# Two of 24 triangular inverses moved from VectorE elimination through DRAM to block doubling on TensorE

## The chip, the cores and the metric

The kernel runs on one core of a Trainium2 chip. A core has five engines that each work through their own instruction stream in order and wait for each other through semaphores: TensorE (PE, with its weight loads PEld), VectorE (DVE), ScalarE (ACT), GpSimd (POOL) and SyncE (SP). SP, ACT and POOL also issue DMAs; a DMA that must wait holds everything behind it in that engine's stream. The metric is the device time in microseconds, where lower is better.

## The reference

Two blocks follow each other. The first is a recurrence (RWKV-7) over 768 tokens for 4 batches and 8 heads with head size 40:

```python
for t in range(S):
    y[:, :, t] = np.einsum('bhd,bhde->bhe', rt, state)
    Sa = np.einsum('bhde,bhe->bhd', state, at)
    state_decay = state * wt[:, :, None, :] - np.einsum('bhd,bhe->bhde', Sa, bt)
    state = state_decay + np.einsum('bhd,bhe->bhde', vt, kt)
```

The second takes the 3072 x 320 result `x` through a feed-forward block: `h = x @ w_in` (1024 wide), `solu = h * softmax(h)`, a layer norm over the 1024 values with gain `g_ln`, and `@ w_out` back to 320. The inputs `w_in`, `w_out` and `g_ln` come as float64 and the kernel gets the two matrices as 64-bit integers.

## The kernel before, in words

The recurrence is cut into chunks of 64 tokens. Within a chunk the effect of `a` and `b` of earlier tokens on later ones is a unit triangular 64 x 64 system for each batch and head, and the chunk needs its inverse. A *step* handles one chunk of two batches, so 16 such systems: there are 24 steps, even ones for batches 0 and 1, odd ones for batches 2 and 3. The systems of a step are independent of the recurrent state, so they can be prepared ahead.

Preparing step i takes, in the order of the code: `load_keys` (w, b, a, k from DRAM), `decay` (L288, logarithm, cumulative sum on PE, two exponentials), `decay_turned` (transposition into `ex`), `scaled` (POOL multiplies b or k by the inverse decay), `front` (L330, transposed `aT`, made by DVE, and `bT`, made by ACT) and `norm` (L351, 16 products on PE, masked by DVE into `nt`, the strictly triangular matrices, and written to DRAM as `nt_dram`).

The inverse is made for a *group* of two steps by `invert` (L379). It reads the two 32 x 32 diagonal blocks of all 32 matrices back from DRAM in another layout (`blk`, `spread`, L370), one block per partition and half, and eliminates column by column on DVE: 30 pairs of a multiply (`prod`, L392) and a subtract (`uu`, L394), each over 128 partitions. The result goes to DRAM (`uu_dram`), and `bring` (L403) loads it back per step as `tu` (one diagonal block) and `uh` (the other). `flip` (L415, a DVE transpose), `couple` (L421, PE product `py`, ACT copy `wy`) and `close` (L434, PE product `pz`, ACT copy into `tu`) then make the full 64 x 64 inverse in `tu[:, :, 32:96]`.

A step's main part follows: `scores` (products of keys, masked by DVE into `psi` and `lv`), `driven` (`px`, the right-hand side), `solved` (`pu`, times the inverse), `answered` (`pl`, masked into `lu`), `read` (`pyo`, output and new state), `leave` (scaling by DVE, and DMAs that turn the output into `xT`). Two to four steps later the feed-forward block of the same tokens runs: `hidden` (product `h`), `exped`, `weighed`, `spreadof`, `folded`, `output`.

The weights are turned from 64-bit floats to 32-bit by DVE and ACT: `land` brings 18 pieces in 13 loads, `narrow(n)` converts the next n pieces (L177 to L191, seven DVE and two ACT instructions a piece). All 18 must be done before `centre_w2` (L207), which runs in step 4.

The order of PE, POOL, DVE and SP is the order of the code. `some(n)` lets n pairs of the oldest unfinished inverse run at that place on DVE. The main loop (L763) starts at i = -1; its body i prepares step i + 5 and does the main part of step i and `scores`, `couple` and `close` of step i + 1. A group takes 30 pairs, so 15 per step are needed; `shares` (L761) and `narrowed` (L762) say where the pairs and the conversions stand in the first bodies. Before the loop the code prepares steps 0 to 3 and does the whole elimination of group 0 (steps 0 and 1, `some(8)`, `some(8)`, `some(14)`) with four conversions among it.

PSUM has three pools: `banks` (two buffers of two banks), `h` (one buffer of two banks) and `bank` (two buffers).

Of the kernel before, what the change touches and what calls it, by code (L numbers as in the profile page):

```python
# [16 lines left out]
P = 128  # L17
# [6 lines left out]
LAG = 1  # L24
LN_EXP = "natural_log_exp_and_others"


def shape_constants():
    s, t = np.arange(P)[:, None], np.arange(P)[None, :]
    same = s // C == t // C  # L30
    row = np.arange(P)[:, None] % C
    parts = dict(
        ident=np.eye(P),
        cum=same & (s <= t),
        tri=row < np.arange(C)[None, :],
        eye_hi=row == Q + np.arange(Q)[None, :],
        neg_hi=-(row >= Q).astype(np.float64),
        mean=np.full((P, P), 2.0 ** -10),
    )
    at, where = 0, {}  # L40
    for name, x in parts.items():
        where[name] = (at, at + x.shape[1])
        at += x.shape[1]
    return np.concatenate([np.asarray(x, np.float64) for x in parts.values()], 1).astype(np.float32), where


@with_exitstack
def kernel(
# [49 lines left out]

    ident, tri = c_("ident"), c_("tri")
# [188 lines left out]
    def decay(i):  # L288
        if not ok(i):
            return  # L290
        d = st[i]
        lw = two.tile([P, DM], FP32, tag="lw", name="lw", bufs=1)
        nc.scalar.activation(out=lw, in_=d["raw_w"].rearrange("p h d -> p (h d)"), func=AF.Ln)
        t = (bank("pcum") if i > 5 else ps2.tile([P, DFF], FP32, tag="h", name="h"))[:, 0:DM]
        nc.tensor.matmul(t, lhsT=c_("cum"), rhs=lw, start=True, stop=True)  # L295
        nc.scalar.activation(out=ei_t[0][:, :, 0:D], in_=heads(t), func=AF.Exp)
        inv = d["inv"] = two.tile([P, DM], FP32, tag="inv", name="inv", bufs=4)
        nc.scalar.activation(out=inv, in_=t, func=AF.Exp, scale=-1.0)
# [52 lines left out]
    def norm(i):  # L351
# [9 lines left out]
        masked(nt, t[:, :, 0:256])  # L361
        n, at = divmod(i, GRP)
# [6 lines left out]

    def spread(n):  # L370
        nb = two.tile([P, Q, Q], FP32, tag="blk", name="blk")
        for y in range(2):
            for e in range(2):
                home = C * y + Q * e
                queue = nc.gpsimd if y and not n else nc.sync
                queue.dma_start(out=nb[home:home + Q], in_=blocks[n][:, Q * e:Q * e + Q, Q * e:Q * e + Q])
# [26 lines left out]
    def bring(i):  # L403
        if not ok(i):
# [10 lines left out]
    def flip(i):  # L415
        if not ok(i):
# [4 lines left out]
    def couple(i):  # L421
        if not ok(i):
# [11 lines left out]
    def close(i):  # L434
        if not ok(i):
# [268 lines left out]
    for i in range(2):  # L704
        load_keys(i, "w")
        load_keys(i, "b", nc.scalar)
        load_keys(i, "a")
    nc.scalar.dma_start(out=g_rows, in_=moe_g_ln.rearrange("(c p) -> c p", p=P))
    load_keys(2, "w")
    for n in range(3):  # L710
        land(n, nc.sync)
    decay(0)
    decay_turned(0)
    for i in range(4):
        scaled(i, "b")
        if i == 3:
            scaled(0, "k")
            scaled(1, "k")
# [4 lines left out]
        if i == 0:  # L723
            load_keys(2, "ba")
        if i == 1:
            load_keys(3, "w")
            begin_inverse(0)
            narrow(3)
            load_keys(3, "ba")
            load_keys(0, "k")  # L730
            load_keys(4, "w")
            some(8)
        if i == 2:
            load_values(0)
            load_keys(1, "k")
            some(8)
    load_keys(5, "w")
    load_keys(4, "ba")
    begin_inverse(1)
    for i in (2, 3):  # L740
        load_keys(i, "k", nc.gpsimd)
    by_value(0)
# [6 lines left out]
    land(3, nc.sync)  # L749
    some(14)  # L750
    narrow(1)
    bring(0)
# [8 lines left out]
    shares = {-1: (0, 8, 6), 0: (0, 9, 7), 1: (0, 9, 6), 2: (0, 9, 6), 3: (0, 9, 6)}  # L761
    narrowed = {-1: (0, 2), 0: (1, 2), 1: (1, 3), 2: (1, 2), 3: (1, 1)}  # L762
    for i in range(-1, N + 3 + LAG):  # L763
# [20 lines left out]
        attend_kv(i + 1)  # L784
        hidden(m - 2, ((1, 1),))
        attend_rs(i + 1)
# [20 lines left out]
        scores(i + 1)  # L807
        if i < 0:
            flip(i + 1)
# [41 lines left out]
```

## Time and profile before

| what | value |
|---|---|
| time, median of 3 runs | 663.46 us (662.66 to 665.79) |
| the profiled execution, its own time | 663.51 us |
| its span, first to last instruction | 661.7 us |
| PE busy | 572.6 us (87%) |
| PEld busy | 408.2 us (62%) |
| DVE busy | 490.0 us (74%) |
| ACT busy | 238.9 us (36%) |
| POOL busy | 216.4 us (33%) |
| elimination pairs on DVE, 12 groups | 108.8 + 107.8 us |
| mean granted TensorE clock | 0.903 |

Busy shares are means over the whole span; the first 200 us and the rest have different limits, so stretches of the span and the chain of waits are read one by one. A row of the timeline has the start, the duration, the engine, the line, the operation and its tiles; a bracket gives the idle time of the engine just before it and what ended that. Matrix products of this kernel are of 32-bit floats and appear as two records each, so 16 products are `x32`.

### The profile page before, as it was taken

To read this page: it belongs to the slowest core of one execution; us is meant where nothing else is said; L and a number is where in the kernel's file an instruction comes from. 1 tells how busy PE (TensorE), PEld (TensorE's weight loads), DVE (VectorE), ACT (ScalarE), POOL (GpSimd) and SP (SyncE) were. 2 spreads that over 40 slices of the span, in tenths; PEclk is the share of its full clock that TensorE was granted. 3 is DMA by queue.
4 is the path that set the end of the run, shared out by engine and by line. 5 is a ranking of instruction groups with operands and counts; after the bars stand their busy time and mean duration, and the time that the engine had idled before them with its cause. 6 is when DMAs were issued, how large, how long until landed. Compare 5 with 4: busy or idle time off the path is not lost.

```text
span 661.7 us, 26730 instructions
## 1 busy us (share of the span) xinstructions
PE 572.6 (87%) x11449; PEld 408.2 (62%) x11449; DVE 490.0 (74%) x1344; ACT 238.9 (36%) x494; POOL 216.4 (33%) x384
## 2 busy tenths in 40 slices
PE   5246674778698999999999999999999999999995
PEld 3134553665565767766776677667766767666653
DVE  4777977888995978888879788888797888423431
ACT  4213333333341443444344334433443233332221
POOL 2342304155050444144315431543244313422200
PEclk9565668659598999999999999999999999999998
DMA  8958976456343645455466465553442412310000
GB/s 165 159 101 132 169 136 106 108 106 124 62 87 62 114 84 108 90 112 107 87 109 114 85 114 89 108 108 77 75 86 58 96 39 48 70 36 26 23 20 20
DMA packets 276749, 59.93 MB, mean 91 GB/s; under 512 B 264656, under 2 KB 274488, under 8 KB 276632
## 3 DMA queue, kind: packets, MB, share of 16 engines
q1 hardware_dynamic: 263384, 44.96, 38.9%
q0 software_dynamic: 7856, 8.76, 5.5%
q10 hardware_dynamic: 5392, 4.51, 2.4%
q8 instruction: 90, 1.47, 0.9%
q14 instruction: 27, 0.22, 0.1%
HBM read 40.10 MB, written 13.37 MB: 81 GB/s over the span
## 4 chain that ended last, share of the span: by engine, by line
PE 73%; DVE 12%; DMA 6%; issue 3%; ACT 2%; SPq 2%; POOL 0%; DVEq 0%; ACTq 0%; POOLq 0%
PE h L232 16%; PE po L680 15%; PE pyo L232 8%; PE ps L232 4%; PE px L232 4%; PE plnT L669 3%; PE pu L232 3%; DVE uu L394 3%; DVE prod L392 3%; PE pk L312 2%; PE pz L232 2%; PE pl L232 2%; PE pcum L295 2%; PE pv L312 2%; PE pnt L232 2%
## 5 line engine op out<-in xcount | busy, mean ns | idle before, releaser
L232 PE MATMUL h<-w_in,xT 128*128 128x512 f32 (+1 forms) x288 | 120.9, 612 | 0.0
L394 DVE TENSOR_TENSOR uu<-uu,prod 128x30 f32<-128x30 f32 (+4 forms) x360 | 108.8, 302 | 12.4
L680 PE MATMUL po<-w,lnT 128*128 128x320 f32 x384 | 115.0, 445 | 3.0 <-DVE w L211 3.0
L392 DVE TENSOR_TENSOR prod<-blk,uu 128x30 f32<-128x30 f32 (+4 forms) x360 | 107.8, 299 | 11.7 <-DMA blk<-nt_dram 1.5
L680 PEld LDWEIGHTS po<-w,lnT 128*128 128x128 f32 x384 | 71.0, 191 | 33.0 <-issue 6.5
L658 POOL TENSOR_TENSOR rs<-c,mhalf 128x1 f32<-128x1 f32 x24 | 13.4, 558 | 194.3 <-DVE c L657 194.3
L600 POOL TENSOR_TENSOR st<-tot,ex 104x160 f32<-104x160 f32 x44 | 21.2, 499 | 135.1 <-DVE tot L596 125.2
L632 DVE TENSOR_REDUCE nmax<-h 128x1 f32<-128x1024 f32 x24 | 29.3, 1221 | 35.6 <-PE h L232 35.6
L232 PEld LDWEIGHTS h<-w_in,xT 128*128 128x128 f32 (+1 forms) x288 | 38.7, 189 | 21.5 <-issue 19.3
L612 POOL DMA_DIRECT2D xT<-x x96 | 48.6, 511 | 0.0
L670 ACT COPY lnT<-plnT 128x512 f32<-128x512 f32 x48 | 26.2, 588 | 43.9 <-PE plnT L669 43.9
L232 PE MATMUL pyo<-lv,kb 64*64 64x104 f32 x768 | 39.1, 277 | 2.7
L232 PE MATMUL pyo<-lu,kb 64*64 64x104 f32 x768 | 37.8, 270 | 0.0
L635 ACT ACTIVATE e<-h,nmax 128x1024 f32<-128x1024 f32 x24 | 26.7, 1113 | 30.5 <-DVE nmax L632 29.4
L431 ACT ACTIVATE wy<-py,cst 128x256 f32<-128x256 f32 x24 | 11.4, 473 | 69.0 <-PE py L232 69.0
L581 DVE TENSOR_TENSOR x<-pyo,ex 104x256 f32<-104x256 f32 x48 | 18.1, 419 | 24.2 <-PE pyo L232 23.2
L254 POOL DMA_DIRECT2D raw_r<-in_r_dram x48 | 34.8, 726 | 1.1 <-issue 1.1
L641 DVE TENSOR_TENSOR e<-h,e 128x1024 f32<-128x1024 f32 x24 | 29.4, 1224 | 7.5 <-ACT e L635 7.2
L649 DVE BATCH_NORM_STATS2 bs<-e 128x6 f32<-128x512 f32 x48 | 30.9, 685 | 0.8
L514 ACT COPY x<-px 128x320 f32<-128x320 f32 x24 | 10.2, 426 | 56.4 <-PE px L232 56.4
L232 PEld LDWEIGHTS ps<-aT,kT 40*64 40x64 f32 x768 | 15.5, 153 | 23.9 <-DVE lu L340 14.3
L684 ACT ACTIVATE osb<-po,rs 128x320 f32<-128x320 f32 x24 | 12.7, 527 | 48.5 <-PE po L680 35.3
(124 smaller groups left out, 1135.5 us busy)
## 6 DMA issues: line engine op xcount, KB each, us to landing
nt_dram<-nt SPq DMA_DIRECT2D x24, 256.0 KB
blk<-nt_dram SPq DMA_DIRECT2D x46, 128.0 KB
raw_w<-in_w_dram SPq DMA_DIRECT2D x48, 80.0 KB
a<-in_a_dram SPq DMA_DIRECT2D x48, 80.0 KB
raw_r<-in_r_dram POOLq DMA_DIRECT2D x48, 80.0 KB, 3.4
lv<-in_v_dram SPq DMA_DIRECT2D x48, 80.0 KB
out_dram<-osb ACTq DMA_DIRECT2D x24, 160.0 KB
raw_b<-in_b_dram SPq DMA_DIRECT2D x44, 80.0 KB
```

What stands on the lines that cost most here:

```text
L232: nc.tensor.matmul(o, lhsT=lhsT, rhs=rhs, start=start, stop=stop, skip_group_check=True)
L254: queue.dma_start(out=x[half(p), :, 0:D], in_=ap[2 * bp + p, :, ci * C:(ci + 1) * C, :].rearrange("h t d -> t h d"))
L312: nc.tensor.transpose(out=t[0:W2, j * P:(j + 1) * P], in_=x[:, 2 * j:2 * j + 2].rearrange("p a b -> p (a b)")[:, 0:W2], identity=ident)
L392: nc.vector.tensor_tensor(out=t, in0=nb[:, j:j + 1, j + 1:Q].to_broadcast([P, n_c, m]), in1=u[:, 0:n_c, j:j + 1].to_broadcast([P, n_c, m]) ...
L394: nc.vector.tensor_tensor(out=u[:, 0:n_c, j + 1:Q], in0=u[:, 0:n_c, j + 1:Q], in1=t, op=ALU.subtract)
L612: nc.gpsimd.dma_start(out=xT[to:to + Q, 2], in_=x[at + P - 3 * D:at + D, 2])
L632: nc.vector.tensor_reduce(out=nmax, in_=d["h"], axis=AX.X, op=ALU.max, negate=True)
L635: nc.scalar.activation(out=e, in_=d["h"], func=AF.Exp, bias=nmax, accum_out=d["esum"])
L641: nc.vector.tensor_tensor(out=d["e"], in0=d["h"], in1=d["e"], op=ALU.mult)
L649: nc.vector.bn_stats(out=bs[:, x], in_=d["e"][:, x * 512:x * 512 + 512])
L670: nc.scalar.copy(out=lnT[:, x * (NF // 2):(x + 1) * (NF // 2)].rearrange("p f t -> p (f t)"), in_=t)
L680: nc.tensor.matmul(d["out"][:, 0:DM], lhsT=d["lnT"][:, f, :], rhs=w2[:, f, :], start=f == 0, stop=f == NF - 1)
```

## The change

Steps 0 and 1 no longer use `invert`, `bring`, `flip`, `couple` and `close`. Instead `double(i)` makes the 64 x 64 inverse of each of the step's 16 matrices by block doubling: with the inverse X of all diagonal blocks of size m = 1, 2, 4, .. 32 at hand, the inverse for size 2m is X times (I minus the lower blocks of N) times X, so that each of six levels is a product `pw` with N (PE), a multiplication by a constant mask (DVE, `w_`), and the products `pxt` and `pxx` that give the transposed and the plain new X. ACT copies `pxt` back to SBUF; `pxx` is copied by DVE in step 0 and by ACT in step 1. The last level leaves out `pxt` and copies `pxx` into `tu` in four quarters, two by DVE and two by ACT. X of both steps lies in the two buffers of `blk`, `w_` in the two buffers of `uu`, `ntm` (N with the identity subtracted) in the two buffers of `psi`.

The two steps' chains alternate at each half level, and the preparation of steps 2 and 3 and part of that of step 0's main part (keys, `scores(0)`) are put between the half levels. The elimination on DVE begins with group 1 (steps 2 and 3), after the chains. Loads before the loop come in another order, two of them on POOL's queue instead of SP's; a table `levels` of 448 columns is loaded on ACT's queue. `decay` always takes its PSUM from `bank`. Two of the four conversions that stood before the loop stand in bodies 2 and 3 now.

```diff
+def doubling_constants():
+    r, c = np.arange(P)[:, None] % C, np.arange(C)[None, :]
+    parts = [r == c]
+    for k in range(DOUBLINGS):
+        m = 2 ** k
+        parts.append(-((r == c) | ((r // m % 2 == 1) & (c // m == r // m - 1))).astype(np.float64))
...
-        t = (bank("pcum") if i > 5 else ps2.tile([P, DFF], FP32, tag="h", name="h"))[:, 0:DM]
+        t = bank("pcum")[:, 0:DM]
...
         masked(nt, t[:, :, 0:256])
+        if i < DOUBLED:
+            d["ntm"] = tokens("psi", 2)
+            nc.vector.tensor_tensor(out=d["ntm"], in0=nt, in1=level(0).to_broadcast([P, 2, 4, C]), op=ALU.subtract)
+            return
...
+        for k in range(DOUBLINGS):
+            y = lambda u: away(u, k)
+            t, w_at = products(banks("pw"), lambda u: d["ntm"][half(on(u)), u[3], 2 * u[1] + u[2]],
+                               lambda u: xt_[xt_at[u]] if k else one(on(u)), on, y)
+            nc.vector.tensor_tensor(out=w_, in0=t, in1=level(k + 1).to_broadcast([P, 2, 4, C]), op=ALU.mult)
+            yield
+            x = lambda u: x_[x_at[u]] if k else one(y(u))
+            last = k == DOUBLINGS - 1
+            if not last:
+                t, xt_next = products(banks("pxt"), x, lambda u: w_[w_at[u]], y, on)
+                nc.scalar.copy(out=xt_, in_=t)
+            t, x_next = products(ps2.tile([P, DFF], FP32, tag="h", name="pxx").rearrange("p (b c) -> p b c", b=2),
+                                 lambda u: w_[w_at[u]], x, y, on if last else lambda u: away(u, k + 1))
+            if last:
+                for at in range(2):
+                    for b in range(2):
+                        copy = nc.scalar.copy if b else nc.vector.tensor_copy
+                        copy(out=tu[half(at), (at ^ b)::2, Q:], in_=t[half(at), b])
+            elif i % 2:
+                nc.scalar.copy(out=x_, in_=t)
+            else:
+                nc.vector.tensor_copy(out=x_, in_=t)
...
+            yield
...
-                queue = nc.gpsimd if y and not n else nc.sync
+                queue = nc.gpsimd if y and n == 1 else nc.sync
...
-    load_keys(2, "w")
-    for n in range(3):
-        land(n, nc.sync)
+    load_keys(2, "b", nc.gpsimd)
+    load_keys(0, "k", nc.gpsimd)
+    load_keys(2, "wa")
+    load_keys(3, "w")
+    load_values(0)
     decay(0)
     decay_turned(0)
-    for i in range(4):
+    for i in range(2):
         scaled(i, "b")
...
+    load_keys(3, "ba")
+    land(0, nc.sync)
+    load_keys(1, "k")
+    load_keys(4, "w")
...
+    chains = [double(i) for i in range(DOUBLED)]
+    for between in (None, front_2, norm_2, front_3, norm_3, None, None, keys_0, None, keys_1, None, lambda: scores(0)):
+        for x in chains:
+            next(x)
+        if between:
+            between()
+    begin_inverse(1)
     load_keys(5, "w")
-    load_keys(4, "ba")
-    begin_inverse(1)
...
-    land(3, nc.sync)
-    some(14)
-    narrow(1)
-    bring(0)
+    for n in (2, 3):
+        land(n, nc.sync)
+    narrow(2)
+    some(6)
...
-    shares = {-1: (0, 8, 6), 0: (0, 9, 7), 1: (0, 9, 6), 2: (0, 9, 6), 3: (0, 9, 6)}
-    narrowed = {-1: (0, 2), 0: (1, 2), 1: (1, 3), 2: (1, 2), 3: (1, 1)}
+    shares = {-1: (0, 8, 4), 0: (3, 6, 3)}
+    narrowed = {-1: (0, 2), 0: (1, 2), 1: (1, 3), 2: (1, 3), 3: (1, 2)}
...
         solved(i)
-        attend_kv(i + 1)
+        if i >= 0:
+            attend_kv(i + 1)
```

The functions between the half levels hold: `front_2` and `front_3` the `front` of steps 2 and 3; `norm_2` the decay of step 3, `norm(2)` and two loads; `norm_3` `norm(3)` and the decay of step 4; `keys_0` and `keys_1` the transposed k, v and r of step 0; the last one `scores(0)`, which is no longer in body -1.

## The prediction

> **What bounds the kernel now.** I read the page's slices first, then busy time by stage, then the chain of waits and the waits of DVE, and last the timeline for prices. The slices:
>
> ```profile
> PE   5246674778698999999999999999999999999995
> DVE  4777977888995978888879788888797888423431
> PEclk9565668659598999999999999999999999999998
> ```
>
> From slice 13 on (about 202 us) PE is full at full clock; before it PE has holes, runs at half clock, and DVE is full. By stage (PE busy, PEld busy, DVE busy, ACT, POOL, granted clock, DMA share, GB/s):
>
> ```profile
> 28.40:54.20 25.80, 10.43 (x93) 7.21 (x92) 21.31 (x66) 4.13 (x9) 12.38 (x17) 0.57 0.72 117
> ...
> 77.00:101.00 24.00, 17.60 (x383) 14.71 (x383) 19.51 (x63) 8.27 (x22) 2.33 (x3) 0.66 0.73 128
> ...
> 126.00:156.00 30.00, 21.70 (x453) 17.12 (x452) 25.04 (x77) 9.91 (x22) 10.10 (x17) 0.63 0.55 114
> ...
> 202.00:224.00 22.00, 21.66 (x415) 14.84 (x416) 13.66 (x43) 6.41 (x13) 7.80 (x14) 0.92 0.38 72
> ```
>
> A body takes 24 to 31 us before 202 us and 22 after. The early bodies carry the conversions on top of 15 pairs, and DVE's "idle" there is mostly the 0.03 to 0.06 us between short instructions. So until about 171 us, where PE's last long hole ends (5.3 us, waiting for DVE's `lu`), a microsecond of DVE is a microsecond of the end; behind that nothing changes. The case is decided by DVE's stream from 17.1 us (the mask `nt` of step 1 done) to there. DVE's true waits, 17 to 202 us (total, times, longest):
>
> ```profile
> DVE psi L340 <- PE ps L232: 6.7, 4, 2.2
> DVE uu L386 <- DMA blk<-nt_dram: 4.9, 2, 3.2
> DVE nt L340 <- PE pnt L232: 4.1, 3, 1.5
> ...
> DVE tu L419 <- DMA tu<-uu_dram: 1.5, 1, 1.5
> DVE prod L392 <- DMA blk<-nt_dram: 1.0, 1, 1.0
> ```
>
> and the trips through DRAM in the chain (start, duration):
>
> ```profile
> 20.39 2.77 DMA nt_dram<-nt
> 23.62 4.20 DMA blk<-nt_dram
> ...
> 95.42 5.76 DMA nt_dram<-nt
> 102.76 3.90 DMA blk<-nt_dram
> ```
>
> Prices of the chain's pieces, at full and at half clock:
>
> ```profile
> 14.97 0.58 ACT L321 COPY bT<-pb 104x512 f32<-104x512 f32 x1 [0.85 <-PE pb L312]
> 15.61 0.69 PE L232 MATMUL pnt<-aT,bT 40*64 40x64 f32 x32 [0.19 <-ACT bT L321]
> 16.38 0.69 DVE L340 TENSOR_TENSOR nt<-pnt,cst 128x512 f32<-128x512 f32 x1 [1.53 <-PE pnt L232]
> ...
> 61.42 1.13 PE L232 MATMUL pnt<-aT,bT 40*64 40x64 f32 x32
> ```
>
> So 16 products of 64 x 64 last 0.69 us, and the next set starts 0.51 us after (`pu` at 73.12 and 73.63); at half clock 1.13 and 0.90. A handoff costs 0.06 to 0.14 us.
>
> **What leaves DVE's stream.** Group 0's 60 pair instructions: the row 28.4 to 54.2 has 21.31 busy, less two `aT` (0.69) and two `nt` (0.69), so 18.6, and 60 gaps of 0.035: 20.7. The group's opening (0.48 + 0.07 + 0.42 + 0.07): 1.1. Two flips: 0.9, and the 1.5 waiting for step 1's `tu`. Waits between 17.1 us and the masks of `scores(0)`: 3.2 for `blk`, 1.3 + 1.2 for `pnt`, 2.2 for `ps`, 0.5 for ACT, together 8.4. The four `aT` and `nt` of steps 2 and 3 (2.8) move into the chains' time. Sum 35.4 us.
>
> **What takes its place.** The chains hold DVE from 17.1 us to the end of `scores(0)`. Their DVE work is 12 masks (0.69), 5 copies (about 0.69), 2 x 0.7 for `ntm`, 4 quarter copies (0.35), so 14.5, and the 2.8 above; the rest is waiting, as no pair or conversion stands between. A level at full clock: `pw` of step 0 issues 0 to 0.51 and lands at 0.69; its mask runs 0.76 to 1.45, that of step 1 to 2.12; PE goes on at 1.55 with `pxt` and `pxx`, `pxt` of step 1 to 3.1; its `pxx` must wait until DVE has emptied the single `h` buffer (copy 2.8 to 3.5), 3.6 to 4.1. So 4.1 us a level, PE busy three quarters. In line: level 0 from 16.9 to 21.1, `front_2` 0.9, level 1 with `norm_2` 4.75, `front_3` 2.0 (its `pb` waits for `ex`, behind three ACT copies), level 2 with `norm_3` 5.2, level 3 4.05, `keys_0` 2.0, level 4 4.05, `keys_1` 0.45, level 5 4.7 (no `pxt`, but four quarter copies in turn before `h` is free), `scores(0)` and step 1's quarters 1.5: end at 50.75, so 33.7 us.
>
> Added to that: the opening loads. `levels` (230 KB) and three loads on POOL's queue (490 KB) now run before step 1's masks, with the DMA share at 0.84 there; `land` goes behind. The logarithm of step 2 stands on ACT ahead of step 1's `bT`, so a late `w` delays the chains: 0 to 3 us, I take 1.0, as 0.7 MB at 163 GB/s is 4.4 us, mostly in the shade of earlier loads. Handoffs not counted, the logarithm of step 4 (its `w` is SP's 12th load, and ACT's chain copies stand behind it) and instruction fetch (one hole of 0.78 us at 99.3 us in dense products): 0 to 3, I take 1.3. Sum 36.0.
>
> **Behind the chains.** `blk` of group 1 lies in the buffers of the chains, so SP holds its reads, and behind them `w` of steps 5 and 6, three `land` and all later loads, until step 0's last product, about 49 us. 4 us later they are there; DVE has 1.4 of masks, 4.9 of conversions and the opening before it looks. PE stands meanwhile at step 5's cumulative sum, which nothing needs before `aT` of step 4, 11 us on. Covered: 0; without the two conversions it would be 2 to 4. POOL's part of `blk` holds the k loads of steps 2 to 4 likewise, same cover.
>
> Group 2: its mask is ready some 35 us after `scores(0)`, near 88 us, and DVE comes to its `blk` at 98. SP issued 47 DMAs from 61.15 to 95.42 us, 0.73 each with waits; it now has 52 from 49 us to that write, so 87. 14 DMAs on SP have gone (2 writes of `nt`, 2 `blk`, 2 `uu_dram`, 8 `tu` and `uh`). From write to last `blk` it took 95.42 to 106.66, so now 99: a wait of 1 to 2 where it was 2.7. Bounds -2.7 and +6 (the old landing kept); I take -0.7.
>
> The conversions are 18 in both. Two run in bodies 2 and 3 instead of ahead of the loop. That in body 3 falls after 171 us, where PE is full: it costs 2.9 if DVE is still late there, 0 if not; I take -0.9 (bounds 0 and -2.9). PE's removed `py` and `pz` (4 sets), `wy` and `tu` copies were in stretches that DVE bounds: 0. ACT's 19 new copies (10 us) are in the chain already.
>
> Sum: 36.0 - 35.4 - 0.7 - 0.9 = -1.0 us. The profiled execution took 663.51, its span 661.7 and 1.8 around it; the median is 663.46, so the two agree. Forecast 662.5.
>
> **The clock.** It decides the chains, and the rows are not kind:
>
> ```profile
> 16.00:18.00 2.00, 0.88 (x27) 0.57 (x16) 1.59 (x5) 1.24 (x4) 0.00 (x0) 1.00 0.98 157
> 18.00:20.00 2.00, 0.00 (x0) 0.00 (x0) 1.85 (x7) 0.43 (x3) 0.00 (x0) 0.60 0.93 182
> ...
> 59.40:62.80 3.40, 3.40 (x43) 2.54 (x42) 2.96 (x14) 2.22 (x5) 0.00 (x0) 0.50 0.20 33
> ```
>
> The clock is full when the chains begin; it fell to 0.50 only 1.5 us after PE's last product (16.9 to 18.4), and later stayed there through 3.4 us of solid PE work. By the third row a clock once lost may stay lost; I take full clock, as the chains leave no such hole. The Trainium skill, "TensorE: Matmul & The Clock Gate", Part 1, says that about 3.4 us of sustained work lifts the clock and an idle window of about 3.4 us drops it; by that the chains stay at full clock, or regain it within a level, and the sum is as above. The same page, in "Wait — 56ns, not 53.3ns?", has a rule against this change: with hardware decode off each matmul costs the sequencer about 62 ns, which by estimate makes 67 us of the chains' 1088 records. The row `pnt` has 32 records in 0.69 us, and I go by the row.
>
> **Rivals.** *Chains at half clock* (ends slower): 34 sets of 0.90, 14 us of PE work between them and two handoffs a level that PE cannot fill: 5.66 a level, end at 61 to 63 us, +10: 672. Speaks for it the third row above; against it that in my walk no hole of PE is over 0.6 us. It decides once the chains end after 56 us, 3.3 us past my 53. *Group 2's `blk` lands no earlier than before* (106.7): DVE waits 8 where it waited 2.7: +6, 668. *All covers hold*: chains at their 33.7 (-1.7), no wait in group 2 (-2.7), the late conversion free (-2): -6.4, 657. *The change does nothing to the end*, since PE bounds the early bodies: against it the 30 us bodies with 21.7 of PE.
>
> **How the numbers follow.** 0.5% is 3.3 us, about what a measurement here can tell from no change. My case (659.2 to 666.8) has 0.42; all covers hold 0.26; half clock or part of it 0.18; group 2 late or the opening loads slower 0.14. The slower cases make 0.32. The range 657 to 671 leaves out a fully cold chain and little else; the likeliest case alone is 659 to 667.
>
> **What would show it.** Right: `scores(0)` masks on DVE at 51 to 55 us; `pw` sets of 0.69; `aT` of step 5 near 80 us (before 77.0), the opening of group 2 at 97 to 99 (before 102.3), `pu` of step 5 within 4 us of 218.7, and bodies of 22 us after. Wrong: sets of 1.1 us in the chains, a first mask `w_` after 19 us, DVE waiting over 3 us for `blk`, or PE holes before `aT` of step 4 that delay it.

## The result, and the profile after

The changed kernel takes 683.0 us (679.5 to 686.1, four executions) beside 663.1 us of the kernel before on the same chip: a ratio of 1.029, 95% interval 1.023 to 1.035. The forecast was 662.5 with a range to 671, so the change is 20.5 us slower than forecast. The profiled execution took 686.12, its span is 684.3; before, the profiled span was 661.7. So the traces below differ by 22.6 us, 2.7 more than the medians.

The first look is at the start of `pu`, the product with the inverse, in each step (from the timeline):

| kernel | step 0 | 1 | 2 | 3 | 4 | 5 |
|---|---|---|---|---|---|---|
| before | 73.12 | 98.32 | 126.30 | 156.72 | 187.27 | 218.66 |
| after | 78.82 | 110.74 | 139.15 | 169.00 | 206.78 | 240.79 |
| later by | 5.7 | 12.4 | 12.9 | 12.3 | 19.5 | 22.1 |

From step 5 on a body takes 22 us as before, and the difference stays. So the loss is made in three places: before step 0, in body 0 (31.9 us from `pu` to `pu` where it took 25.2), and in bodies 3 and 4 (37.8 and 34.0 where they took 30.6 and 31.4).

The slices of the page after (40 equal parts of the span):

```profile
PE   4874536759577899999999999999999999999995
DVE  3536977597599597887878888869888878433432
PEclk9997556567669999999999999999999999999998
```

DVE was at 7 to 9 in nearly all of the first 12 slices before; now it stands at 3, 5 and 3 in the first three slices, and drops to 5 in three later ones. Busy time by stretch (length, then busy time of PE, PEld, DVE, ACT, POOL, granted clock, DMA share, GB/s), from the end of step 1's `nt` to the first mask of `scores(0)`, then bodies -1, 0 and 3:

```profile
21.00:61.60 40.60, 30.55 (x1256) 25.80 (x1248) 16.68 (x27) 15.63 (x32) 6.95 (x11) 0.96 0.34 70
61.60:79.00 17.40, 9.71 (x99) 6.64 (x102) 16.18 (x42) 5.65 (x14) 10.75 (x15) 0.52 0.98 168
79.00:111.00 32.00, 15.35 (x331) 12.83 (x331) 24.37 (x75) 9.38 (x26) 3.32 (x5) 0.57 0.75 129
...
169.00:207.00 38.00, 26.34 (x479) 18.62 (x482) 28.45 (x87) 11.93 (x24) 9.39 (x17) 0.69 0.33 64
```

The chains last 40.6 us, and DVE works in 16.7 of them. The clock is 0.96 there, so this is not the cold chain of the first rival. In body 3 DVE is idle for 9.5 of 38 us. What DVE waited for from 17 to 240 us (total, times, longest):

```profile
DVE bits L201 <- ACT scale L192: 12.7, 3, 6.7
DVE psi L353 <- PE ps L245: 11.1, 4, 5.3
DVE w__311 L423 <- PE pw L245: 9.3, 5, 3.4
DVE both L440 <- PE pxx L245: 6.2, 5, 2.2
DVE nt L353 <- PE pnt L245: 5.6, 5, 2.7
DVE lu L353 <- PE pl L245: 2.7, 1, 2.7
```

Rows 3 and 4 are the chains' own waits. The first row was 2.2 us before (three waits, 0.9 the longest); no step of the prediction has it. No wait for `blk` is left, where the forecast had left 1 to 2 us of it in group 2. Part of that is luck: DVE opens group 2 at 113.84 us, not at 97 to 99, so a later landing would not have been noticed either.

### The profile page after: what moved, and what is told of

The parts are those of the page before. It is cut to its first block, busy times and chain, and to the rows that moved or that the text cites. A ratio compares the mean times of both kernels' runs of the same rounds, so it can differ in the third digit from the quotient of the medians.

```text
span 684.3 us, 28630 instructions
## 1 busy us (share of the span) xinstructions
PE 590.7 (86%) x12409; PEld 420.8 (61%) x12409; DVE 484.1 (71%) x1301; ACT 246.2 (36%) x509; POOL 219.4 (32%) x388
## 4 chain that ended last, share of the span: by engine, by line
PE 57%; DVE 4%; DMA 4%; issue 2%; SPq 2%; ACT 1%; DVEq 0%; ACTq 0%
PE h L245 14%; PE po L757 13%; PE pyo L245 6%; PE px L245 3%; PE ps L245 3%; PE plnT L746 3%; PE pu L245 3%; DMA blk<-nt_dram 2%; PE pl L245 2%; PE pz L245 1%; PE pk L325 1%; PE pv L325 1%; PE pr L325 1%; PE pst L540 1%; PE py L245 1%
## 5 line engine op out<-in xcount | busy, mean ns | idle before, releaser
L245 PE MATMUL h<-w_in,xT 128*128 128x512 f32 (+1 forms) x288 | 122.7, 622 | 0.0
L469 DVE TENSOR_TENSOR prod<-blk,uu 128x30 f32<-128x30 f32 (+4 forms) x330 | 99.1, 300 | 12.5 <-DMA blk<-nt_dram 3.3
L471 DVE TENSOR_TENSOR uu<-uu,prod 128x30 f32<-128x30 f32 (+4 forms) x330 | 98.8, 300 | 11.3
L712 ACT ACTIVATE e<-h,nmax 128x1024 f32<-128x1024 f32 x24 | 26.7, 1113 | 32.9 <-DVE nmax L709 32.0
L308 PE MATMUL pcum<-lw,cst 128*128 128x320 f32 x48 | 23.6, 579 | 13.7 <-ACT lw L306 8.0
L658 DVE TENSOR_TENSOR x<-pyo,ex 104x256 f32<-104x256 f32 x48 | 18.1, 419 | 23.9 <-PE pyo L245 23.0
L325 PE MATMUL pv<-cst,v 128*104 128x128 f32 x96 | 16.5, 299 | 17.3 <-POOL v L298 16.9
L349 DVE TENSOR_TENSOR aT<-pa,ex 104x512 f32<-104x512 f32 x24 | 16.5, 687 | 19.7 <-PE pa L325 10.6
```

What stands on the lines that cost most here:

```text
L245: nc.tensor.matmul(o, lhsT=lhsT, rhs=rhs, start=start, stop=stop, skip_group_check=True)
L325: nc.tensor.transpose(out=t[0:W2, j * P:(j + 1) * P], in_=x[:, 2 * j:2 * j + 2].rearrange("p a b -> p (a b)")[:, 0:W2], identity=ident)
L469: nc.vector.tensor_tensor(out=t, in0=nb[:, j:j + 1, j + 1:Q].to_broadcast([P, n_c, m]), in1=u[:, 0:n_c, j:j + 1].to_broadcast([P, n_c, m]) ...
L471: nc.vector.tensor_tensor(out=u[:, 0:n_c, j + 1:Q], in0=u[:, 0:n_c, j + 1:Q], in1=t, op=ALU.subtract)
L712: nc.scalar.activation(out=e, in_=d["h"], func=AF.Exp, bias=nmax, accum_out=d["esum"])
```

## The experiments

Each time is a median over four to ten executions, beside the kernel before on the same chip (662.97 for e1 to e4, 663.37 for e5 to e7, 663.46 for e8 to e10, 663.16 for e11 and e12).

### The order of the pairs in bodies 0 to 3

The diff had also put three pairs ahead of `carried`, `driven` and `front`, which the prediction did not price.

```diff
-    shares = {-1: (0, 8, 4), 0: (3, 6, 3)}
+    shares = {-1: (0, 8, 4), 0: (0, 9, 3), 1: (0, 9, 6), 2: (0, 9, 6), 3: (0, 9, 6)}
```

> The changed kernel, in which bodies 0 to 3 take no pairs ahead of carried, driven and front and nine behind (0, 9) where it takes three and six; the number of pairs per body is the same. Theory A (the end is late because the chains end late: +3.9 us at the opening and +7 in the chains, and everything behind only carries that): 681.5 to 684.5, no more than 1.5 from the changed kernel. Theory B (about half of the loss is made behind the chains: with three pairs first, DVE comes to the conversions while ACT still stands in a row of copies that wait for PE, so DVE waits for ACT's scale, 12.7 us in all, 6.7 the longest): those waits fall below 5 us in all, and the time to 674 to 678.

Measured: 674.99 us (672.1 to 676.0), ratio 1.018 (1.016 to 1.021): 8.0 us less than the changed kernel. The two traces lie 14.0 us apart (spans 684.3 and 670.3), as the profiled execution of the changed kernel was its slowest and that of this run its fastest; differences between them are larger than the typical ones. DVE's waits in the same stretch:

```profile
DVE w__311 L423 <- PE pw L245: 7.9, 5, 3.4
DVE psi L353 <- PE ps L245: 7.4, 4, 3.7
DVE bits L201 <- ACT scale L192: 5.3, 3, 3.5
```

`pu` starts at 77.39, 106.02, 130.24, 159.91, 192.79 and 226.75 us, so bodies 0, 1 and 3 are 3.3, 4.2 and 4.9 us shorter. Theory B holds by the time; the waits for `scale` stay at 5.3 us, where less than 5 was expected. 8 of the 20 us belong to the order of the pairs, not to the doubling.

How three pairs do this can be followed in body 3 of the changed kernel. With them, and a group's opening in front, `aT` runs at 175.56, 6.6 us behind `pu`; in the experiment it runs 2.3 us behind. PE has a hole of 4.25 us (3.41 in the experiment) before `pv`, which waits for POOL's copy of v. The granted clock in three stretches of body 3, after (first fence) and in the experiment (second), PE busy first:

```profile
171.00:174.00 3.00, 0.00 (x0) 0.00 (x0) 2.60 (x9) 0.61 (x2) 1.82 (x4) 1.00 0.54 101
174.00:177.00 3.00, 2.02 (x6) 1.38 (x7) 2.74 (x10) 0.59 (x1) 1.31 (x3) 0.51 0.42 94
177.00:180.00 3.00, 2.32 (x9) 1.30 (x7) 2.69 (x12) 0.58 (x1) 0.00 (x0) 0.50 0.59 94
```

```profile
161.00:164.00 3.00, 0.63 (x8) 0.38 (x4) 2.67 (x8) 1.40 (x3) 1.80 (x4) 1.00 0.54 101
164.00:167.00 3.00, 1.97 (x7) 1.01 (x8) 2.62 (x12) 0.59 (x1) 1.37 (x3) 0.81 0.40 94
...
170.00:174.00 4.00, 2.51 (x72) 1.72 (x70) 0.58 (x3) 2.04 (x6) 0.00 (x0) 1.00 0.55 95
```

After the hole PE goes on at half clock in the changed kernel and stays there; in the experiment the clock is back within 9 us. ACT's copies `vT`, `rT`, `s` and `ex` each wait for a PE set, and the conversion's `scale` stands behind them on ACT, with DVE waiting for it. ACT and DVE of the changed kernel:

```profile
176.11 0.59 ACT L334 COPY vT<-pv 104x512 f32<-104x512 f32 x1 [4.50 <-PE pv L325]
...
183.53 0.58 ACT L341 COPY ex<-pei 104x512 f32<-104x512 f32 x1 [2.50 <-PE pei L325]
...
186.70 0.47 ACT L192 ACTIVATE scale<-scale 128x320 int32<-128x320 int32 x1
```

```profile
187.20 0.49 DVE L201 SCALAR_TENSOR_TENSOR bits<-bits,scale 128x320 int32<-128x320 int32 x1 [6.65 <-ACT scale L192]
```

That the order costs 8 us is shown; that it does so through this hole and the clock is read from traces and was not tried by itself. Three more runs keep the changed kernel's order: e2_loads and e3_own_buffers, with holes of 4.20 and 4.24 us before `pv`, take 37.8 us for body 3, like the changed kernel; e5_levels, with a hole of 3.31, takes 35.5. So of the 4.9 us some 2.3 go with the length of the hole, and the other 2.6 with the order in a way that was not followed.

The same reordering was made in the kernel before:

```diff
-    shares = {-1: (0, 8, 6), 0: (0, 9, 7), 1: (0, 9, 6), 2: (0, 9, 6), 3: (0, 9, 6)}
+    shares = {-1: (0, 8, 6), 0: (3, 6, 7)}
```

> The kernel before, with only the order of the pairs changed in bodies 0 to 3: three ahead of carried, driven and front and six behind, where it has none and nine. No chain, no new load. Theory A: within 1.5 of 663. Theory B: DVE's waits for ACT's scale, 2.2 us before, rise to 8 or more, and the time to 668 to 672.

Measured: 666.51 us (664.6 to 668.3), ratio 1.005 (1.004 to 1.007): +3.5 us. Neither number was met: the order costs there too, but less than half, and the waits for `scale` are 5.7 us in two rows (3.1 for `bits`, 2.6 for `w`), not 8. In the changed kernel bodies 2 and 3 carry one conversion more each; that the order costs more for that reason is a guess that no run tried.

### The opening loads

```diff
-    load_keys(2, "b", nc.gpsimd)
-    load_keys(0, "k", nc.gpsimd)
-    load_keys(2, "wa")
-    load_keys(3, "w")
-    load_values(0)
+    load_keys(2, "w")
...
+        if i == 0:
+            load_keys(2, "ba")
+            load_keys(3, "w")
     load_keys(3, "ba")
+    load_keys(0, "k")
+    load_values(0)
```

> The changed kernel with the opening loads in the old order: b of step 2, k of step 0 and r of step 0 are no longer issued on POOL at the start, w of step 2 is the last load ahead of step 0, and b, a of step 2 and w of step 3 are issued after step 0's mask. levels stays where it is. Theory A: the mask nt of step 1 is done at 17.1 to 18 us where it was 20.98, nothing later waits for the moved loads, and the time falls by 3 to 4: 679 to 680. If levels (230 KB) alone makes the opening late, nt of step 1 stays behind 20 us and the time within 1. If the moved loads are missed later, the chains grow by what the opening gains (front_2 waits for b of step 2), and the time stays too.

Measured: 681.6 us (679.6 to 682.6), ratio 1.027 (1.025 to 1.030); `nt` of step 1 is done at 20.9 us, as in the changed kernel. So the order of the loads by itself does not bring the opening forward. The first logarithm and ACT's queue of this run:

```profile
5.47 0.63 ACTq L785 DMA_DIRECT2D levels<-levels  x1
6.89 0.74 ACTq L786 DMA_DIRECT2D g_rows<-in_moe_g_ln_dram  x1
7.68 0.47 ACT L306 ACTIVATE lw<-raw_w 128x320 f32<-128x320 f32 x1 [5.66 <-DMA raw_b<-in_b_dram]
...
14.32 1.13 PE L245 MATMUL pnt<-aT,bT 40*64 40x64 f32 x32
```

The bracket names a load, but the logarithm starts 0.05 us after ACT has issued `g_rows`; before, it stood at 6.14, 0.05 behind the same issue. The load of `levels` has been put into ACT's stream ahead of the first work that ACT has. And PE's sets, which before were at 0.69 from 12.2 us, are at 1.13 until 19 us. It does not follow that the moved loads cost nothing. In the changed kernel the logarithm of step 1 comes after a wait for which the profile shows no releaser,

```profile
12.31 0.47 ACT L306 ACTIVATE lw<-raw_w 128x320 f32<-128x320 f32 x1 [2.07 <-issue]
```

and in e2_loads it stands at 10.32 without a wait; but there PE's sets stay long until 19 us, where the changed kernel has them at 0.60 to 0.69 from 17.2, and the two cancel. The next run moves the one issue of `levels` as well; no run moves it alone.

```diff
-    nc.scalar.dma_start(out=levels, in_=nc.inline_tensor(doubling_constants(), name="levels").ap())
+    nc.gpsimd.dma_start(out=levels, in_=nc.inline_tensor(doubling_constants(), name="levels").ap())
```

> The loads of e2_loads, and levels issued on POOL's queue instead of ACT's. In e2_loads the first logarithm stands at 7.68 us behind the issue of levels and of g_rows on ACT (5.47 to 7.63), where the kernel before has it at 6.14, and PE's sets stay at half clock (pnt 1.13 us) until 19 us, where before they are at 0.69 from 12.2. Theory E (ACT's 1.5 us of issuing, and by it a later rise of the clock, is what made the opening late): first logarithm at 6.1 to 6.3, pnt of step 0 at 0.69, nt of step 1 done by 17.5, and the time 677.5 to 679, 3 to 4 under e2_loads. Rival (the bytes of levels, 224 KB, take the place of the w and b loads): nt of step 1 stays behind 19.5 us and the time within 1 of e2_loads.

```profile
6.17 0.47 ACT L306 ACTIVATE lw<-raw_w 128x320 f32<-128x320 f32 x1 [4.14 <-DMA raw_w<-in_w_dram]
...
12.79 0.69 PE L245 MATMUL pnt<-aT,bT 40*64 40x64 f32 x32
...
17.37 0.69 DVE L353 TENSOR_TENSOR nt<-pnt,cst 128x512 f32<-128x512 f32 x1 [1.55 <-PE pnt L245]
```

Beside e2_loads only this issue has moved, so it is shown that it held the first logarithm: logarithm at 6.17, sets at 0.69 from 12.79 us, `nt` done at 18.1 (17.5 was expected) instead of 20.9, with the same bytes. In the traces everything behind is earlier by as much (the first mask of `scores(0)` by 3.3 us, the span 677.3 beside 680.8). The time was 680.1 us (675.1 to 681.6), ratio 1.025 (1.019 to 1.030): only 1.5 less than with `levels` on ACT's queue, where 3 to 4 were expected; single executions of this kernel lie 6 us apart, so the size is not settled better than that.

### Buffers of the chains

SP is in order, and its reads of `blk` of group 1 waited for the chains' buffers; this row of SP's queue shows it in the changed kernel:

```profile
SPq L453 <- DVE both L440: 13.2, 1, 13.2
...
SPq L453 <- PE pxx L245: 4.3, 1, 4.3
```

The prediction had the wait, and priced what stands behind it at 0. In the run the chains get other buffers:

```diff
-        both = two.tile([P, Q, Q], FP32, tag="blk", name="both")...
+        both = two.tile([P, Q, Q], FP32, tag=("e", "lnT")[i], name="both", bufs=1)...
-        w_ = two.tile([P, Q // 2, Q], FP32, tag="uu", name="w_")...
+        w_ = two.tile([P, Q // 2, Q], FP32, tag=("nuT", "x")[i], name="w_", bufs=1)...
```

> The changed kernel, in which the chains' x, its transpose and w_ lie in the buffers of e, lnT, nuT and x, which nothing else uses yet, instead of blk and uu. So SP and POOL are not held at blk of group 1 from 40.3 to 57.8 us; the scheduler also puts ACT's part of the two conversions behind the logarithm and the exponentials of step 5. Cover holds (the prediction's term of 0: DVE has masks and conversions until blk is there, and what PE waits for at step 5's cumulative sum is needed later): within 1 of 683. Theory D (the hold costs: w of step 5 is 17 us late, ACT's lw and PE's pcum of step 5 and all behind it in body -1 follow): aT of step 5, 30.6 us behind the mask psi of step 0, comes 3 us earlier, and the time is 678 to 680.

Measured: 679.65 us (677.5 to 681.2), ratio 1.024 (1.021 to 1.027): 3.4 us less, in theory D's range. PE stood in the changed kernel for the logarithm of step 5 (in order behind the conversions on ACT, whose `land` is late) and then for `aT` of step 5:

```profile
PE pk L325 <- DVE aT L349: 12.9, 1, 12.9
...
PE pcum L308 <- DMA bits<-in_moe_w_in_dram: 5.7, 1, 5.7
```

The start of step 5's cumulative sum, forecast as needed by nobody for 11 us, moves from 66.88 to 62.8 us. But the sign that theory D named is not there: `aT` of step 5 stands at 92.44 us, where the changed kernel has it at 92.17, and PE now waits 9.1 us for `aT` of step 4. `pu` of step 0 is later than in the changed kernel (83.4 against 79.3 for its second half) and that of step 1 earlier by 3.7, as the scheduler also moved ACT's part of the conversions. Nor are the new buffers free, as was expected: `land` fills `e` and `lnT` too, and SP now waits for the chains at these loads (L173, 6.9 and 4.5 us). So 3.4 us belong to this edit; on which path they were won stays open.

The three changes together (order, loads with `levels` on POOL's queue, buffers):

> e1_order, e3_own_buffers and e5_levels together. If DVE's stream bounds all of it, the gains add: 683.0 - 8.0 - 3.4 - 4.5 = 667, 665 to 669. If they cover the same wait (the earlier start only makes the next engine's lateness show), 670 to 674. Still slower than before in both cases, as the chains' 40 us stand in place of 35 us of DVE's work.

Measured: 671.94 us (670.7 to 673.6), ratio 1.014 (1.011 to 1.017). The gains don't add: 11.1 where the three runs brought 8.0, 3.4 and 2.9. And it is still 8.6 us slower than before. What is left is not these three. Other parts of the diff were never run alone, among them the PSUM of `decay` and the two conversions moved into bodies 2 and 3.

### The chains' idle time, filled

In e6_three DVE still works only 15.85 us of the 41.2 from 18.8 to 60.0 us, which is the chains but for their first microsecond. The next run puts work there: the conversions become a generator that stops after each DVE instruction, and group 1 starts among the last levels. For this the load of the third and fourth piece (`land(1)`) moves ahead of the chains, and bodies 2 and 3 carry no more conversions than in the kernel before.

```diff
+    for n, between in enumerate((None, front_2, norm_2, front_3, norm_3, None, None, keys_0, None, keys_1, None, ...)):
         for x in chains:
             next(x)
+            if n == 11 and x is chains[0]:
+                some(1)
...
+        if 1 <= n <= 6:
+            fill((4, 2, 4, 4, 4, 6)[n - 1])
+        if n == 4:
+            begin_inverse(1)
+        if n > 6:
+            some((1, 1, 2, 1, 0)[n - 7])
-    narrow(2)
-    some(6)
+    narrow(1)
...
-    narrowed = {-1: (0, 2), 0: (1, 2), 1: (1, 3), 2: (1, 3), 3: (1, 2)}
+    narrowed = {-1: (0, 2), 0: (1, 2), 1: (1, 3), 2: (1, 2), 3: (1, 1)}
```

> e6_three, and DVE's waits in the chains (17 us in the changed kernel) are filled: half of the first four conversions' instructions are put between the half levels, 24 of 28, so that two conversions fewer stand behind the chains and two fewer in bodies 2 and 3, and group 1's opening and first six pairs stand between the last half levels instead of behind scores(0). If DVE bounds the stretch and its waits in the chains are free: 10 us of DVE's work leaves the stretch behind the chains, 3 to 5 come back as a longer chain: 660 to 663, 5 to 7 under e6_three. Rival (the chains' critical path runs over DVE and ACT, each inserted instruction delays it): within 2 of e6_three.

Measured: 661.35 us (659.4 to 662.5, ten executions), ratio 0.997 (0.995 to 0.999): 10.6 us less than e6_three, and 2.0 less than before. The time is in the expected range, but the gain is not: it is 10.6 for 5 to 7, as e6_three had come out 5 us slower than the 667 expected of it. The stretch of the chains in e6_three and in this run:

```profile
18.80:60.00 41.20, 29.62 (x1226) 24.80 (x1227) 15.85 (x27) 15.57 (x32) 13.72 (x19) 1.00 0.55 111
```

```profile
18.80:62.00 43.20, 30.75 (x1219) 26.16 (x1223) 29.69 (x66) 18.37 (x39) 14.52 (x19) 0.94 0.52 107
```

13.8 us of DVE's work went in. From the end of step 1's mask to the first mask of `scores(0)` it is 42.1 us in e6_three (17.84 to 59.91) and 44.7 here (17.83 to 62.48), so the chains grew by 2.6. `pu` starts at 72.83, 97.05, 124.15, 153.84, 184.41 and 215.79 us: earlier than before in every step, and DVE's waits for `scale` are 2.2 us, the longest 0.9, as before.

Which half of the filling does it? Without the pairs (they stand behind `scores(0)` again):

> e7_filled without the pairs in the chains: group 1's opening and six pairs stand behind scores(0) again, as in e6_three; the conversions' 24 instructions stay between the half levels. 24 instructions of some 0.36 are 8.6 us, the opening and six pairs 5.5 us, 14.1 together, of which 10.6 were gained. If both halves pay alike: 671.9 - 10.6 x 8.6/14.1 = 665.4, 664 to 667. If the conversions are nearly free in the chains and the pairs delay them: 661 to 663. If the conversions delay the chains and the pairs bring the gain: 668 or more.

Measured: 662.91 us (660.5 to 667.8), ratio 0.999 (0.997 to 1.002), in the range of the second case. The conversions alone bring 9.0 of the 10.6 us; the pairs bring 1.6, where their work is 5.5, and as the intervals of the two runs overlap that may be nothing.

The starts of `pu` show where the gain is made:

| kernel | step 0 | 1 | 2 | 3 | 4 | 5 |
|---|---|---|---|---|---|---|
| before | 73.12 | 98.32 | 126.30 | 156.72 | 187.27 | 218.66 |
| e6_three | 77.53 | 102.51 | 126.72 | 156.32 | 189.19 | 225.63 |
| e9_conversions | 73.67 | 98.60 | 125.90 | 153.72 | 186.67 | 218.07 |
| e7_filled | 72.83 | 97.05 | 124.15 | 153.84 | 184.41 | 215.79 |

e6_three starts 4.4 us late in step 0, but in step 3 it is level with the kernel before; its 7 us in step 5 are made in bodies 3 and 4 (32.9 and 36.4 us for 30.6 and 31.4), behind the two conversions that the diff had moved into bodies 2 and 3. The filling takes these back as well. So the 10.6 us are not all idle time of the chains that was put to use: in the traces 2.5 of the gain is there in step 3, and 7.4 comes in bodies 3 and 4. Moving the two conversions back without filling the chains was not tried.

### The end of the chains, and a fuller filling

```diff
-            t, x_next = products(ps2.tile([P, DFF], FP32, tag="h", name="pxx")...
+            t, x_next = products(banks("pxx") if last else ps2.tile([P, DFF], FP32, tag="h", name="pxx")...
...
-                        copy = nc.scalar.copy if b else nc.vector.tensor_copy
-                        copy(out=tu[half(at), (at ^ b)::2, Q:], in_=t[half(at), b])
+                        nc.scalar.copy(out=tu[half(at), (at ^ b)::2, Q:], in_=t[half(at), b])
```

> e7_filled, with the last product of each step in a bank of its own instead of the single buffer h, and all eight quarter copies on ACT instead of by turns on DVE and ACT. In e7_filled the quarters go DVE, ACT, DVE, ACT, each behind the other, and step 1's last product waits for them (in the changed kernel 1.77 us on PE). If the end of the chains still bounds DVE there: PE's wait goes, DVE loses four copies of 0.43 and 1.8 of waits, the time falls by 2 to 3: 658.5 to 659.5. Rival (ACT's eight copies stand ahead of step 5's logarithm or scores' wait for PE stays): within 1 of 661.4.

Measured: 658.4 us (656.1 to 658.9), ratio 0.992 (0.989 to 0.995): 3.0 less than e7_filled, as expected, and the fastest version found. It beats the kernel before by 5 us. From the end of step 1's mask to the first mask of `scores(0)` it takes 40.1 us (19.41 to 59.50), with DVE busy in 29.1.

> e8_last_copies with the chains filled further: all 28 instructions of the first four conversions, three of them ahead of step 3's aT, where DVE waits 2.0 for ex, and eight pairs instead of six, one more in the wait of 1.6 ahead of level 4's mask and one in the 1.8 ahead of scores(0). The body -1 takes two pairs fewer. If those waits are free: four conversion instructions (1.5) and two pairs (1.2) leave the stretch behind: 655.5 to 657. If the chains' critical path already runs over DVE: 658 to 660.

Measured: 658.98 us (657.7 to 659.7), ratio 0.993 (0.990 to 0.995): no gain over e8_last_copies, as the second case had it. The same stretch takes 42.9 us here (18.12 to 61.02). That fits chains whose own path runs over DVE, but it does not show it: the granted clock in the stretch is 0.92, where e8_last_copies has 1.00.

### PE's holes in the chains

The prediction allowed 1.3 us for handoffs, the late logarithm of step 4 and instruction fetch together. In the changed kernel PE's holes without a releaser (the profile shows nothing that PE waited for) alone sum to 4.1 us (1.60, 0.75, 1.04, 0.48, 0.25), of which three:

```profile
25.35 0.28 PE L245 MATMUL pxx<-levels,w__311 64*64 64x64 f32 x3 [1.60 <-issue]
...
42.15 0.27 PE L245 MATMUL pxt<-w__331,both 64*64 64x64 f32 x1 [0.75 <-issue]
...
45.88 0.27 PE L245 MATMUL pxt<-w__311,both 64*64 64x64 f32 x1 [1.04 <-issue]
```

Between the last two lie 128 records of PE (1 and 32 of the two sets at 42.15, 64 of `pw`, 31 of `pxt`), and in the other runs the holes stood at products of one list, 126 to 128 records apart or a multiple of that, though not every place of the list has a hole in every run. So a period of 128 records was suspected. The pages have a number that fits it: the packets of the DMA queue of kind instruction, before (11449 matmul records) and in the changed kernel (12409),

```profile
q8 instruction: 90, 1.47, 0.9%
q8 instruction: 98, 1.61, 1.0%
```

are one for every 127 matmul records in both. To see what the holes belong to, products were added at the start.

```diff
+    t = bank("pw")
+    for _ in range(64):
+        mm(t[0:C, 0:C], idle[0:C], idle[0:C])
     decay(0)
```

> e7_filled with 64 more products of 64 x 64 on zeros at the very start, where PE stands idle until the first logarithm; their result is not used. In all runs PE's holes without a releaser in the chains (0.25 to 2.2 us, 4 to 7.5 us in all) stand at the same products and 127 or 128 products apart. Theory F (PE fetches its instructions in blocks of 128 products with their weight loads): every hole now stands 64 products earlier in the chains' order, 128 apart as before; the time moves by no more than 2 either way, as other sets are hit. Rival (the holes belong to those products, to their data or to the transfers at that time): they stay at the products of e7_filled. The 64 products may also raise PE's clock earlier in the opening (sets of 0.65 instead of 1.09 before 12 us); then the mask nt of step 1 comes up to 2 us sooner, and the time falls by that.

This run could not answer: 64 products are 128 records, a whole period, and its holes stood at products where earlier runs have them. Its time was 669.36 us (667.0 to 670.9), ratio 1.009 (1.006 to 1.012), 8.0 above e7_filled, as the 64 products took 13.92 us and held the first cumulative sum until 14.84. By accident that shows what lateness at the opening costs: `nt` of step 1 is done at 25.6 instead of 17.8 us, 7.8 later, and the end comes 8.0 later by the medians and 6.8 by the two traces. All engines start late there, so it does not tell DVE from the others. Half as many products, over four quarters:

```diff
+    t = banks("pw")
+    for n in range(32):
+        x, y = half(n % 2), half(n // 2 % 2)
+        mm(t[y, x.start // C, 0:C], idle[x], idle[x])
     decay(0)
```

> e7_filled with 32 products on zeros at the very start, whose result is not used, turned over four quarters in two banks as the chains' are. Each product has two records in the trace, so the 64 of e10_shift were 128 records, a whole period of the holes, and could not tell the theories apart; 32 products are half a period. At half clock they last 2.3 us (32 records took 1.13), from 1 to 3.5 us, before the first logarithm at 6.2: the opening stays where it was. Theory F (PE fetches its instructions in blocks of 128 records with their weight loads): the holes of e7_filled, before the last 15 records of pw of level 1, the last 18 of pxt of step 1 in level 1, the last of pxt of step 1 in level 2 and the last of pxt of step 0 in level 3, go 64 records up: to pxt of step 0 in level 1 (18 left), pxt of step 0 in level 2 (1 left), pw of level 3 (33 left). Rival (the holes belong to those products or to the transfers at that time): they stay. Time within 2 of 661.4 in both cases.

Holes of e7_filled (first fence), and of this run (second):

```profile
26.67 0.46 PE L259 MATMUL pw<-both,psi 64*64 64x64 f32 x15 [2.18 <-issue]
...
30.50 0.50 PE L259 MATMUL pxt<-w__334,both 64*64 64x64 f32 x18 [0.74 <-issue]
...
43.33 0.27 PE L259 MATMUL pxt<-w__314,both 64*64 64x64 f32 x1 [0.94 <-issue]
```

```profile
23.69 0.34 PE L261 MATMUL pxx<-levels,w__369 64*64 64x64 f32 x6 [1.51 <-issue]
...
30.18 0.80 PE L261 MATMUL pxt<-w__349,both 64*64 64x64 f32 x18 [1.81 <-issue]
...
43.10 0.73 PE L261 MATMUL pw<-both,psi 64*64 64x64 f32 x33 [0.25 <-issue]
...
46.83 0.27 PE L261 MATMUL pxt<-w__369,both 64*64 64x64 f32 x1 [1.06 <-issue]
```

Two of the four went 64 records up, to the products named beforehand: from step 1's `pxt` of level 1 to step 0's (both with 18 left), and from the last of step 0's `pxt` of level 3 to `pw` with 33 left. The hole before the last 15 records of `pw` of level 1 went 63 records up, to step 1's `pxx` of level 0 with 6 left. The fourth, named for step 0's `pxt` in level 2, shows no hole there. The last row, which was not named, stands 128 records behind the one before it. So the holes go by the count of PE's instructions, not by the products or the data. That they are waits for fetched instructions fits this and the packets of the instruction queue; no run shows it directly. The time was 662.03 us (659.8 to 663.9), ratio 0.997 (0.995 to 0.999), no different from e7_filled.

## Why the prediction was wrong

Its premise held where it was tried, in the opening: 7.8 us of lateness there came out as 8.0 (e10_shift), and the bodies from step 5 on take 22 us. Right too: sets of 0.69 us in most of the chains; group 2's `blk` costs no wait any more (2.7 before; the forecast took 0.7 of it), by luck in part, as said above; no cold chains (clock 0.96 in 21.0 to 61.6, so the first rival fell, though the chains end at 62.9, where it had put them: the sign named for it, an end after 56, could not tell a slow clock from other causes). The signs of being right were missed: masks of `scores(0)` at 61.6 us for 51 to 55, `aT` of step 5 at 92.2 for 80, group 2's opening at 113.8 for 97 to 99, `pu` of step 5 at 240.8 for 218.7. Of the signs of being wrong, a first mask `w_` after 19 us (21.88) and PE holes ahead of `aT` were there.

Against the rule of the Trainium skill that with hardware decode off each matmul costs some 62 ns ("TensorE: Matmul & The Clock Gate", "Wait — 56ns, not 53.3ns?"): 1256 records of PE, those of the preparation included, ran within 40.6 us, and 32 in 0.69, so the row decided rightly. No run here shows which way of decoding was on. The rule of its Part 1, that the clock falls after an idle window of about 3.4 us, does not fit here. In the stretch of the first hole PE was busy 0.00, 0.65 and 0.66 us of three successive microseconds, and the next rows are

```profile
27.00:28.00 1.00, 1.00 (x20) 0.93 (x10) 0.00 (x0) 0.58 (x1) 0.00 (x0) 0.63 0.00 0
28.00:29.00 1.00, 1.00 (x9) 0.65 (x11) 0.69 (x1) 0.00 (x0) 0.00 (x0) 0.50 0.00 0
29.00:30.00 1.00, 1.00 (x40) 1.00 (x44) 0.00 (x0) 0.58 (x1) 0.00 (x0) 0.50 0.00 0
```

at half clock, though no hole was longer than 1.6 us.

Four steps failed. The first rests on two rows of the changed kernel, step 1's mask, where the chains begin, and the second mask of `scores(0)`, where they end:

```profile
20.29 0.69 DVE L353 TENSOR_TENSOR nt<-pnt,cst 128x512 f32<-128x512 f32 x1 [1.55 <-PE pnt L245]
...
62.20 0.68 DVE L353 TENSOR_TENSOR lv<-ps,cst 128x512 f32<-128x512 f32 x1
```

- *Chains, 36.0 from 17.1 to the end of the masks of `scores(0)`.* From 17.1 to 62.9 it is 45.8 us, so 9.8 too little was taken. Of these, 2.9 are the opening (3.9 measured, 1.0 taken, bound 3): the prediction weighed bytes, and what e5_levels shows is the issue of `levels` on ACT ahead of the first logarithm, and sets that stayed long with it. (The profile's granted clock reads 1.00 in all of the opening, so that a low clock made them long is not shown.) Some 2.8 are the term for handoffs, logarithm and fetch: 4.1 of holes alone against 1.3, if all of them lie on the path. Some 1.6 are PE's sets at half clock behind the hole of 1.60 (`pa` 1.00 and `pb` 1.06 for 0.60, 64 records of `pw` in 1.95 for 1.16). The last 2.5 were not split; step 1's last product, which waited 1.77 for the quarter copies, is among them. With the opening mended the chains are still too long: in e6_three the mask is done at 17.84 and the second mask of `scores(0)` at 61.2, 44.1 us from 17.1, with 6.5 us of such holes.
- *"I take -0.9" for the two conversions moved into bodies 2 and 3.* A gain was taken, 2.9 us at the most, since PE was held to be full in body 3. Bodies 3 and 4 take 9.9 us more than before in the changed kernel, 4.9 in e1_order and 7.4 in e6_three, which starts them no later than the kernel before; in e7_filled, where bodies 2 and 3 carry as many conversions as before, they take what they took (e9_conversions, the same with its pairs elsewhere: 2.4 more). As no run moved the conversions alone, this is read from the traces and not shown by an experiment.
- *"Covered: 0" for the loads behind the chains' buffers.* 3.4 us (e3_own_buffers). The cover named DVE's masks and conversions and PE's cumulative sum; ACT is not in it, where step 5's logarithm stood behind conversions that were themselves late. Whether that is the path of the 3.4 us stays open.
- *A step that is missing: the place of the pairs.* The numbers in `shares` were read for how many pairs a body takes, which hardly changes, and not for what stands in front of `aT`. 8.0 us (e1_order).

These sizes are not parts of one sum, though 9.8, 8.0 and 3.4 come near the 20.5: the first is read from a trace of the slowest execution, e6_three shows that the gains overlap by some 3 us, and the loss in bodies 3 and 4 lies partly in the 8.0.

*"The rest is waiting, as no pair or conversion stands between"* is no wrong term, as the waiting is in the 36.0. But it was entered as a cost that cannot move: 40.6 us in which DVE works 16.7, for 35.4 us of which 9.9 were waits. Filling it, and taking the two conversions out of bodies 2 and 3 with that, brought 10.6 us (e7_filled).

## What to carry to other kernels

When serial work on one engine is replaced by a chain over several, the chain must be priced by its whole length, and its idle time on the bounding engine counts as a loss until other work of that engine is written into it; here the version that did so went from 671.9 to 661.4 us. A diff that also moves "neutral" things (which queue issues a load, where pairs and conversions stand in an in-order stream) has to be read stream by stream: here the order of the pairs alone cost 8.0 us. A DMA issued on a computing engine ahead of its first instruction can hold that instruction: here the first logarithm stood at 7.68 us with it and at 6.17 without, with the same bytes moved.

## What the runs showed of the hardware that was not expected

- PE stops for 0.25 to 2.2 us at places 126 to 128 matmul records apart, with their weight loads, mostly where the products come densely (32 records in some 0.5 us). The holes are there with the DMA engines almost idle too: 1.04 us in e5_levels at 41.60, in a stretch (40 to 50 us) with a DMA share of 0.02.
- 64 products of 64 x 64 that all use one quarter of the array and one target took 13.92 us, 0.109 us a record; 32 that go by turns over four quarters and two banks took 1.98, 0.031 a record, at the same place in the program.
- The profile shows a granted clock of 1.00 in the opening, while sets last twice their later time (`pcum` 1.43 us at 14.84 in e10_shift, after 13.9 us of unbroken PE work; 0.81 at 19.59).
- DVE's conversion instructions are longer beside POOL's: in e8_last_copies three of them take 0.67, 0.97 and 0.94 us where they took 0.42, 0.42 and 0.28 otherwise, from 42.8 to 45.4 us, when POOL copies v and r and multiplies k (43.21 to 45.19). That was seen, and not tried by itself.
